# Attention and a state-space convolution on one core: transfers planned with their issue time, K's first weights moved, zero matmuls that fill every loop step

## The chip, the cores and the metric

The kernel runs on one core of a Trainium2 chip. The metric is the device time of one execution in microseconds (us), taken as the median of several runs. TensorE (PE) multiplies matrices, VectorE (DVE) and ScalarE (ACT) work on elements, GpSimd (POOL) sets a few buffers, and SyncE (SP) does nothing here but issue transfers. SP's own queue is shown as SPq.

## The reference

Two branches work on the same x (2048 positions, 512 channels) and are mixed by a gate:

```python
g = sigmoid((x * gate_w).sum(-1, keepdims=True))
# a: attention, 32 heads of 16 channels
q, k, v = split(x @ wqkv); p = softmax(q @ k.T * 16**-0.5); a = (p @ v) @ wo
# b: diagonal state-space convolution, 128 states per channel
dt = exp(log_dt); P = exp(dt * (A_re + 1j*A_im) * l)          # l = 0..2047
K = einsum("dn,dnl,dn->dl", C, P, dt * B).real
b = causal_convolution(x, K) + x * Dskip
return g * a + (1 - g) * b
```

## The kernel before

**The loop.** Attention is a loop of 683 steps over score tiles of 128 x 1536 (three of 128 x 512 each). Step t issues one exponential on ACT (`ex`, L679 to L682, the instruction at L681 that reads a score buffer SC and writes ET), and on TensorE the score matmuls for step t + 2 (`fill`, L661). SC has two buffers, so ACT has one tile in hand while TensorE fills the next. Value matmuls (`pv`, L684) accumulate into OA. One block of heads takes 16 key tiles, some 21 steps; then OA is moved out by VectorE (`norm`, L700) before the next block may open it. ET holds six tiles, so value matmuls can lag a little.

**The convolution** is done in chunks of 64 positions, as side work between the attention's instructions, by generators ("threads") with priorities: `params` and `bases` compute powers on VectorE; `table` writes tables PT and stores them to HBM; `qload` (L895, transfer at L899) reads them back transposed into Qt; `sstage` multiplies Qt with blocks of x into the PSUM bank MB, VectorE moves MB to Sst (L937), a transfer (L940) stores it, and `sload` (L960) reads it back transposed into SG; `scan` runs the recurrence on VectorE (L979 to L989); `kstage` makes the convolution kernels (Kst, stored at L917); `yload` (Py at L1004, four Tt loads at L1009) and `ystage` make the output from Tt, Py and SG in MB, stored at L1050 and read back transposed at L1065; `combine` and `outs` gate it and add the output projection. MB is one bank under a lock: a thread asks for it, works, and hands it back (`unlock`) as soon as the eviction to VectorE has been issued in the plan.

**The planner.** The order of all instructions is fixed when the program is built. `Prog.put` (L174) appends an operation to its engine's list and books its start and end on a model of the engines: `c` is its duration (for a transfer, time from issue to landing), `LAT` the delay of a semaphore. For a transfer the queue is booked like this (L194):

```python
if o.dma:
    self.free[eng] = t + .12
    e = t + o.c
```

`Sched.run` (L311) looks in each step for side operations whose operands are due in time by that model and appends them. TensorE, VectorE and the queues then run their lists in order on the chip: an operation that waits holds back all behind it on its engine.

**Zero matmuls.** `keep` (L696) multiplies zeros (the buffer wm) and adds them to OA, so that TensorE stays at work. At the end of each step they are appended until the step's TensorE work (`sch.units`) reaches 3.2 units of some 0.22 us, if a value accumulation is open (`opened`) and the model has room:

```python
while opened and sch.units < 3.2 and p.free["PE"] + .3 < lim:
    put(keep((pvn - 1) // 16))
    sch.units += 1
```

**Head.** Before the loop, ACT's queue issues x's first rows (x0n), log_dt (ldt), and the first columns of the weights Wk and Wq; SP's queue issues the transposed loads AreT and AimT, then Wv and the rest. TensorE runs nine zero matmuls, transposes x0n (L1181), ACT and VectorE copy the result to xT (L1192), then the first projections follow. ACT also computes dt, ea, e2 and a sine and cosine (L1193 to L1202) ahead of the loop.

**Placement.** `place` (L450) gives every buffer its bytes; buffers whose lifetimes in the plan don't meet may share bytes, and then the later one waits for the earlier one's last use.

Of the kernel before, what the change touches and what calls it, by code (L numbers as in the profile page):

```python
# [12 lines left out]
P = 128  # L13
# [54 lines left out]
class Prog:  # L68
# [179 lines left out]
class Sched:  # L248
# [62 lines left out]
    def run(self, now, pe_end, dve_end, margin=.02):  # L311
        p = self.p
        self.control()
        while True:
            best = None
            holder = [t for t in self.thr if t in self.lock.values()]
            for th in holder + [t for t in self.thr if t not in holder]:
                ops = th[3]
                if ops is None or isinstance(ops, tuple):
                    continue  # L320
                r = p.ready(ops)
                if r is None:
                    continue
                eng = ops[0].eng
                f = p.free[eng]
                if ops[0].dma:
                    if r > pe_end:
                        continue
                    k = 0
                elif eng == "PE":  # L330
                    c = sum(o.c for o in ops)
                    if max(f, r) + c > pe_end:
                        continue
                    k = 0 if r <= f + .03 else 2
                elif eng == "DVE":
                    if max(f, r) > dve_end:
                        continue
                    k = 0 if r <= f + .03 else 1 if r <= f + .16 else 2
                else:
                    if r > now:  # L340
                        continue
                    k = 0
                key = (k, r if k == 2 else 0)
                if best is None or key < best[0]:
                    best = (key, th)
                if k == 0:
                    break
# [102 lines left out]
def place(nc, bufs):  # L450
# [3 lines left out]

    def fit(order):
        done, top = [], base
        for b in order:
            n = (b.nbytes() + 31) // 32 * 32
            busy = sorted((o.lo, o.hi) for o in done if o.first <= b.last + 1 and b.first <= o.last + 1)
            at = base  # L460
            for lo, hi in busy:
                if at + n <= lo:
                    break
                at = max(at, hi)
            b.lo, b.hi = at, at + n
            top = max(top, b.hi)
            done.append(b)
        return top
# [3 lines left out]
    def rnd():  # L472
        nonlocal seed
        seed = (seed * 1103515245 + 12345) % 2 ** 31
        return seed / 2 ** 31

    best = None
    for k in range(200):
        def rank(b):
            w = rnd() * (0 if k < 2 else .8)  # L480
            return (-(b.last - b.first > 300) if k % 2 else 0, -b.nbytes() * (1 + w * 2) * (b.last - b.first + 20) ** (w if k >= 2 else 0))
        order = sorted(sbs, key=rank)
        top = fit(order)
        if best is None or top < best[0]:
            best = (top, order)
        if best[0] <= end:
            break
    for k in range(3000):
        if best[0] <= end:
            break  # L490
        order = list(best[1])
        order.insert(int(rnd() * len(order)), order.pop(int(rnd() * len(order))))
        top = fit(order)
        if top <= best[0]:
            best = (top, order)
    assert best[0] <= end, (best[0] - end, live(sbs))
    fit(best[1])
# [35 lines left out]
def record(p, B, ins):  # L533
# [21 lines left out]
    def dma(eng, fn, R, W, c):  # L555
        return O(eng, fn, R, W, c, dma=True)
# [10 lines left out]
    def load_xT(c):  # L567
        return dma("SP", lambda e: e.dma_start_transpose(xT(512 * c, [[S, 4], [1, 512]]),
                                                         dap(x_t, 512 * c * D, [[D, 512], [1, D]])), [], [(xT, c)], [0, 9, 15, 18][c])

    def load_par(n, src, c):
        return dma("SP", lambda e: e.dma_start_transpose(B[n](0, [[1, D]]), src), [], [(B[n], 0)], c)

    def load_w(n, c0, at, cols, sl, eng, c):
# [9 lines left out]
        load_w("Wv", 2 * D, 0, D, 0, "SP", 10),  # L584
        load_xT(1),
        load_w("Wk", D, P, D - P, 1, "SP", 15),
        load_w("Wq", 0, P, D - P, 1, "SP", 16),
        load_xT(2),
        load_xT(3))
    for n, s in (("BreT", "bre"), ("BimT", "bim"), ("CreT", "cre"), ("CimT", "cim")):  # L590
        put(load_par(n, ins[s], 24))
    put(dma("SP", lambda e: e.dma_start(B["gwT"](0, [[1, 4]]), dap(ins["gw"], 0, [[1, P], [P, 4]]), allow_slow_non_contiguous=True),
            [], [(B["gwT"], 0)], 27))
    for a in range(4):
        put(dma("SP", lambda e, a=a: e.dma_start(B["Dpb"](0, [[1, 16]], 32 * a, 32), dap(ins["dsk"], 0, [[1, 16], [256, 2], [16, 16]]),
                                                 allow_slow_non_contiguous=True), [], [(B["Dpb"], a)], 28))
# [156 lines left out]
    def params():  # L753
# [49 lines left out]

        yield [tt(full("u1"), half(L1, 0), full("e2"), ALU.mult, key("L1", "e2"), key("u1"))]
# [51 lines left out]
    def table():  # L856
# [5 lines left out]
        for pb in range(NBLK // 2):  # L862
# [21 lines left out]
            for i, blk in enumerate(blks):  # L884
                yield [dma("SP", lambda e, i=i, blk=blk: e.dma_start(ptd.dram(blk * P * PTN, [[PTN, P], [1, PTN]]), PT(i * PTN, [[1, PTN]])),
                           [W[i]], [(ptd, blk)], 6.0)]
# [8 lines left out]
    def qload(blk):  # L895
        if blk >= 2:
# [3 lines left out]
                                                         ptd.dram(blk * P * PTN, [[PTN, P], [1, PTN]])), [(ptd, blk)], [(Qt, blk % 2, blk)], 9.0)]  # L900
        sch.add(sstage(blk), 7)

    def kstage(blk):
# [4 lines left out]
        for part, wn in ((0, "wrb"), (1, "nwi")):  # L908
# [9 lines left out]
                   [(Kst, blk % 2, blk), (Kst, "z")], [(kpd, blk)], 4.5)]  # L918
# [4 lines left out]
    def sstage(blk):  # L923
        q0, qr, bl = (blk % 2) * PTN, blk // 4, blk % 4
        for bank in range(4):
            yield ("LOCK", "MB")
            os = []
            for pp in range(2):
                for j in range(4):
# [12 lines left out]
                       [(sd, (blk, bank))], 3.0)]  # L942
# [5 lines left out]
    def sload(blk):  # L948
# [7 lines left out]
        if bl == 0:  # L956
            yield [pool(lambda g: g.memset(sg(0, [[1, 2 * RS]]), 0.0), [], [(sg, "z")], 256)]
            if qr < 2:
# [3 lines left out]
                   [(sd, (blk, i)) for i in range(4)], [(sg, bl, (qr, 'S'))], 7.0)]  # L962
# [38 lines left out]
    def yload(u):  # L1001
# [4 lines left out]
                   [(ptd, blk)], [(Py, r, u)], 6.0)]  # L1006
        for par in range(2):
            for a in range(2):
# [3 lines left out]
                           [(kpd, blk)], [(Tt, (r, par, a), u)], 5.0)]  # L1012
        sch.mark(f"yl{u}")

    def ystage():
        def unit(u):
# [11 lines left out]
            for qq in range(2):  # L1028
# [9 lines left out]
                for q in (2 * qq, 2 * qq + 1):  # L1038
                    for ri in range(2):
# [11 lines left out]
                       [(Yst, r2, u)], [(ytd, u)], 2.6)]  # L1051
# [12 lines left out]
    def yread(blk):  # L1064
        yield [dma("SP", lambda e: e.dma_start_transpose(Yl(CB * blk, [[D, 16], [1, CB]]), ytd.dram(CB * blk * S, [[S, CB], [1, S]])),  # L1065
                   [(ytd, 2 * blk), (ytd, 2 * blk + 1)], [(Yl, blk)], 3.6)]
# [3 lines left out]
    def ublocks():  # L1070
# [3 lines left out]
        for qr in range(4):  # L1074
            yield ("Q", 30 + 10 * qr)
            for par in range(2):
                yield [dma("SP", lambda e, qr=qr, par=par: e.dma_start(X2(2048 * qr, [[64, 32], [1, 64]], 64 * par, 64),
                                                                       B["xrd"].dram(64 * qr + 256 * par, [[32 * D, 64], [D, 32], [1, 64]])),
                           [(B["xrd"], 0)], [(X2, (qr, par))], 7)]
# [45 lines left out]
    def out_st(lt):  # L1125
        return dma("SP", lambda e: e.dma_start(dap(ins["out"], 128 * lt * D, [[D, P], [1, D]]), fo((lt % 4) * D, [[1, D]])),
                   [(fo, lt % 4)], [(B["d_out"], lt)], 2.5)
# [65 lines left out]
    put(O("ACT", lambda a: a.activation(B["dt"](0, [[1, D]]), B["ldt"](0, [[1, D]]), AF.Exp), key("ldt"), key("dt"), .55))  # L1193
    put(tt(full("an"), full("AreT"), full("dt"), ALU.mult, key("AreT", "dt"), key("an")),
# [4 lines left out]
        O("ACT", lambda a: a.activation(B["e2"](0, PERM), B["an"](0, NAT), AF.Exp, scale=-2.0), key("an"), key("e2"), .55),  # L1199
# [37 lines left out]
    def pvs(t, limit):  # L1237
        nonlocal pvn, opened
        done = 0
        while pvn < NQ and (4 * pvn + 3) // W3 <= t and done < 2:  # L1240
# [19 lines left out]
            if not must and (r is None or r > p.free["PE"] + .03 or p.free["PE"] + .33 > limit):  # L1260
# [13 lines left out]
    for t in range(NT):  # L1274
# [27 lines left out]
        while opened and sch.units < 3.2 and p.free["PE"] + .3 < lim:  # L1302
            put(keep((pvn - 1) // 16))
# [5 lines left out]
    while True:  # L1309
        pvs(NT, 1e9)  # L1310
        if pvn >= NQ - 1:
            break
    sch.run(1e9, 1e9, 1e9)
# [47 lines left out]
```

## Time and profile before

| what | us |
|---|---|
| median of 3 runs (lowest, highest) | 1022.89 (1021.15, 1026.08) |
| the profiled execution | 1019.5 |
| its span, first to last instruction | 1017.4 |
| TensorE busy | 890.5 |
| ScalarE busy | 934.6 |
| VectorE busy | 605.8 |
| mean granted TensorE clock | 0.906 of full |

The busy times are unions over the whole span; they don't say which engine ended the waits in which stage. In views by stage each row has the stretch, its length, the busy time of each engine with its number of instructions, the granted clock, the share of the DMA engines and the rate. In the list of waits a row reads: who waited, for whom, total, times, longest. In rows in order of time: start, duration, engine, line, operation, tiles, count, and in brackets the idle time ahead and what ended it.

### The profile page before, as it was taken

To read this page: it belongs to the slowest core of one execution; us is meant where nothing else is said; L and a number is where in the kernel's file an instruction comes from. 1 tells how busy PE (TensorE), PEld (TensorE's weight loads), DVE (VectorE), ACT (ScalarE), POOL (GpSimd) and SP (SyncE) were. 2 spreads that over 40 slices of the span, in tenths; PEclk is the share of its full clock that TensorE was granted. 3 is DMA by queue.
4 is the path that set the end of the run, shared out by engine and by line. 5 is a ranking of instruction groups with operands and counts; after the bars stand their busy time and mean duration, and the time that the engine had idled before them with its cause. 6 is when DMAs were issued, how large, how long until landed. Compare 5 with 4: busy or idle time off the path is not lost.

```text
span 1017.4 us, 17925 instructions
## 1 busy us (share of the span) xinstructions
PE 890.5 (88%) x7623; PEld 261.4 (26%) x7623; DVE 605.8 (60%) x1315; ACT 934.6 (92%) x694; POOL 8.4 (1%) x17
## 2 busy tenths in 40 slices
PE   7999998889888888698899885988998999888887
PEld 2222222222222222122122332324233222222222
DVE  6999899972289998399972214799861420000001
ACT  6999999999799999699999964899897999999996
POOL 2000000000000000000000000000000000000000
PEclk9999989989799999889788965699795999999999
DMA  8710000076448417761653689835516100000000
GB/s 180 142 25 1 1 1 1 1 207 181 84 139 223 115 48 181 200 117 42 191 154 91 175 182 186 170 73 120 131 34 135 42 27 1 1 1 1 1 1 21
DMA packets 227406, 92.25 MB, mean 91 GB/s; under 512 B 191872, under 2 KB 215040, under 8 KB 225280
## 3 DMA queue, kind: packets, MB, share of 16 engines
q1 hardware_dynamic: 225600, 90.21, 37.0%
q10 hardware_dynamic: 1728, 0.92, 0.4%
q8 instruction: 59, 0.97, 0.4%
q14 instruction: 19, 0.16, 0.1%
HBM read 27.92 MB, written 35.65 MB: 62 GB/s over the span
## 4 chain that ended last, share of the span: by engine, by line
ACT 50%; PE 17%; DVE 15%; SPq 10%; DMA 5%; issue 1%; ACTq 0%; DVEq 0%
ACT ET L681 48%; PE OA L547 8%; PE SC L547 5%; PE MB L547 4%; SPq L1009 3%; DVE tt L712 3%; ACT EX L681 2%; DMA Qt<-gm_ptd 2%; SPq L960 2%; SPq L899 2%; DMA Tt<-gm_kpd 2%; DVE G L987 2%; DVE Sst L937 1%; DVE s L981 1%; DVE s L985 1%; DVE PT L712 1%
## 5 line engine op out<-in xcount | busy, mean ns | idle before, releaser
L681 ACT ACTIVATE ET<-SC 128x1536 bf16<-128x1536 f32 x665 | 902.8, 1598 | 68.1 <-PE SC L547 67.4
L547 PE MATMUL SC<-Qm,KT 32*128 32x512 bf16 x2048 | 285.3, 412 | 68.5 <-ACT ET L681 49.6
L547 PE MATMUL OA<-wm 128*128 128x512 bf16 x1015 | 324.6, 409 | 1.2 <-DVE wm L606 1.2
L547 PE MATMUL OA<-ET,VE 128*32 128x512 bf16 x1994 | 212.1, 420 | 0.0
L547 PEld LDWEIGHTS SC<-Qm,KT 32*128 32x128 bf16 x2048 | 67.0, 92 | 357.1 <-ACT ET L681 281.2
L702 DVE STREAM_TRANSPOSE OT<-OA 128x512 f32<-128x512 f32 x32 | 22.8, 713 | 193.6 <-PE OA L547 193.5
L547 PEld LDWEIGHTS OA<-wm 128*128 128x128 bf16 x1015 | 65.7, 99 | 132.6 <-issue 118.6
L937 DVE TENSOR_TENSOR Sst<-MB,sgn 128x512 bf16<-128x512 f32 x64 | 43.9, 686 | 65.9 <-PE MB L547 39.1
L547 PEld LDWEIGHTS OA<-ET,VE 128*32 128x32 bf16 x1994 | 51.1, 94 | 124.4 <-issue 120.8
L712 DVE TENSOR_TENSOR tt<-B,D 128x1024 bf16<-128x1024 bf16 x96 | 62.0, 680 | 0.5
L987 DVE TENSOR_TENSOR G<-s,s 128x256 f32<-128x256 f32 x120 | 50.5, 421 | 3.0
L1048 DVE CAST Yst<-MB 128x256 bf16<-128x256 f32 x32 | 13.5, 423 | 64.6 <-PE MB L547 59.5
L981 DVE TENSOR_TENSOR s<-G,MU 128x256 f32<-128x256 f32 x120 | 49.9, 416 | 0.1
L983 DVE TENSOR_TENSOR s<-G,MU 128x256 f32<-128x256 f32 x120 | 49.9, 416 | 0.0
L985 DVE TENSOR_TENSOR s<-s,SG 128x256 f32<-128x256 f32 x120 | 49.8, 415 | 0.0
L547 PE MATMUL MB<-Qt,X 64*32 64x256 bf16 x512 | 31.5, 326 | 18.7 <-DVE Sst L937 12.3
L547 PE MATMUL MB<-Tt,X 64*32 64x64 bf16 x512 | 25.1, 246 | 25.4 <-DMA Tt<-gm_kpd 24.5
L989 DVE CAST SG<-G 128x256 bf16<-128x256 f32 x120 | 34.7, 289 | 3.2
L712 DVE TENSOR_TENSOR ft<-FP,L 128x1024 f32<-128x1024 f32 (+1 forms) x32 | 33.7, 1082 | 0.4
L712 DVE TENSOR_TENSOR PT<-tt,tt 128x1024 bf16<-128x1024 bf16 x48 | 32.7, 682 | 0.6
L547 PE MATMUL MB<-Py,SG 128*32 128x64 bf16 x1024 | 29.6, 244 | 0.0
L547 PEld LDWEIGHTS MB<-Tt,X 64*32 64x32 bf16 x512 | 15.7, 145 | 48.5 <-DMA Tt<-gm_kpd 32.7
(131 smaller groups left out, 423.0 us busy)
## 6 DMA issues: line engine op xcount, KB each, us to landing
gm_ptd<-PT SPq DMA_DIRECT2D x16, 1024.0 KB, 5.7
Py<-gm_ptd SPq DMA_DIRECT2D x32, 512.0 KB, 4.5
gm_sd<-Sst SPq DMA_DIRECT2D x64, 128.0 KB, 1.8
gm_kpd<-Kst SPq DMA_DIRECT2D x16, 256.0 KB, 3.5
Tt<-gm_kpd SPq DMA_DIRECT2D x128, 32.0 KB, 3.6
gm_xrd<-in_A_x_dram SPq DMA_DIRECT2D x1, 2048.0 KB, 11.8
X<-gm_xrd SPq DMA_DIRECT2D x8, 256.0 KB, 6.1
gm_ytd<-Yst SPq DMA_DIRECT2D x32, 64.0 KB, 2.5
```

The source lines that it names most:

```text
L547: return O("PE", lambda t: t.matmul(out(), lhsT(), rhs(), start=start, stop=stop, skip_group_check=True, **kw), R, W, c, l, u)
L681: return ac(lambda a: a.activation(b(1536 * e, [[1, 512 * n]]), sc(0, [[1, 512 * n]]), AF.Exp, scale=DH ** -0.5), [(sc, k, (t, k)) for k i ...
L702: yield [dv(lambda v: v.transpose(OT(0, [[1, 512]]), OA(0, [[1, 512]])), [(OA, 0, b)], [(OT, 0, b)], 560)]
L712: return dv(lambda v: v.tensor_tensor(o(), a(), b_(), f), R, W, n, k)
L899: yield [dma("SP", lambda e: e.dma_start_transpose(Qt((blk % 2) * PTN, [[128, 32], [1, 128]]), ptd.dram(blk * P * PTN, [[PTN, P], [1, PTN] ...
L937: yield [dv(lambda v, bank=bank: v.tensor_tensor(Sst(512 * bank, [[1, 512]]), MB(0, [[1, 512]]), sgn(0, [[1, 512]]), ALU.mult), [(MB, 0, ( ...
L981: yield [dv(lambda v: v.tensor_tensor(s2(0, V2), G(0, V2), MU(d0, [[0, 2], [1, 128]]), ALU.mult), key("G", "MU"), [(s2, 0)], 256)]
L983: yield [dv(lambda v: v.tensor_tensor(s3(0, V2), G(128, [[-128, 2], [1, 128]]), MU(D + d0, [[D, 2], [1, 128]]), ALU.mult), key("G", "MU") ...
L985: yield [dv(lambda v, so=so: v.tensor_tensor(s2(0, V2), s2(0, V2), sg(so, [[RS, 2], [1, 128]]), ALU.add), [(s2, 0)] + ks, [(s2, 0)], 256)]
L987: yield [dv(lambda v: v.tensor_tensor(G(0, F), s2(0, F), s3(0, F), ALU.add), [(s2, 0), (s3, 0)], [(G, 0)], 256)]
L989: yield [dv(lambda v, so=so: v.tensor_copy(sg(so, [[RS, 2], [1, 128]]), G(0, V2)), key("G"), last, 256, 2)]
L1009: yield [dma("SP", lambda e, par=par, a=a: e.dma_start(Tt(r * 512 + 256 * a, [[64, 4], [1, 64]], 64 * par, 64), kpd.dram(blk * P * 8 * P + ...
```

## The change

- The model of a queue: every transfer books its queue for a time `u` of its own kind (0.6 us by default) in place of 0.12 us for all, and most landing times `c` are set anew. A transfer is only appended when the modelled queue is free by the end of the step. `emit` counts `u` as TensorE work for TensorE's operations alone.
- `ready` refuses a write into a place that holds something not yet read.
- Head: Wk's first columns go to SP's queue, ahead of AreT and AimT; Wq's move up to third on ACT's. Five zero matmuls are put behind the transposes of x0n. On ACT, dt's exponential goes ahead of the two copies; e2 is no longer an exponential of ACT, but a product and a reciprocal on VectorE, in `params` after the mark "D48".
- `keep` can also write into MB, as a matmul of its own. A step is topped up to 3.2 units when an accumulation is open, as before, and now also when none is open and nobody holds MB.
- At the end, value matmuls are appended without regard to the model's time, and side work is run between them.
- `place` searches for a placement in another way.

```diff
-                for b, sl, *_ in acc:
+                for b, sl, *tag in acc:
...
+                    if wr and tag and not st[1] and b.tags.get(sl, "warm") not in ("warm", tag[0]):
+                        return None
...
-            self.free[eng] = t + .12
+            self.free[eng] = t + o.u
...
-            self.units += o.u
+            if o.eng == "PE":
+                self.units += o.u
...
-                    if r > pe_end:
+                    if max(r, f) > pe_end:
...
-    def dma(eng, fn, R, W, c):
-        return O(eng, fn, R, W, c, dma=True)
+    def dma(eng, fn, R, W, c, u=.6):
+        return O(eng, fn, R, W, c, u=u, dma=True)
...
-        load_w("Wk", D, 0, P, 0, "ACT", 6.8),
-        load_w("Wq", 0, 0, P, 0, "ACT", 8.0),
+        load_w("Wq", 0, 0, P, 0, "ACT", 6.5),
+        load_w("Wk", D, 0, P, 0, "SP", 7.0),
...
     def keep(b):
-        return mm(lambda: OA(0, [[1, 512]]), lambda: wm(0, [[1, P]]), lambda: wm(0, [[1, 512]]), [(wm, 0)], [(OA, 0, b)],
-                  False, False, c=.24)
+        o = MB if b is None else OA
+        return mm(lambda: o(0, [[1, 512]]), lambda: wm(0, [[1, P]]), lambda: wm(0, [[1, 512]]), [(wm, 0)],
+                  [(o, 0, "warm" if b is None else b)], b is None, b is None, c=.24)
...
+        yield [tt(perm("u1"), nat("ea"), nat("ea"), ALU.mult, key("ea"), key("u1"))]
+        yield [dv(lambda v: v.reciprocal(B["e2"](0, [[1, D]]), B["u1"](0, [[1, D]])), key("u1"), key("e2"), 3050)]
...
-    put(copy_dve(*cp[0]), copy_act(*cp[1]), copy_dve(*cp[2]), copy_act(*cp[3]))
+    put(*[mm(lambda: OA(0, [[1, 512]]), lambda: wm(0, [[1, 128]]), lambda: wm(0, [[1, 512]]), [(wm, 0)], [(OA, 0, "warm")], c=.22)
+          for k in range(5)])
+    put(copy_dve(*cp[0]), copy_dve(*cp[2]))
     put(O("ACT", lambda a: a.activation(B["dt"](0, [[1, D]]), B["ldt"](0, [[1, D]]), AF.Exp), key("ldt"), key("dt"), .55))
+    put(copy_act(*cp[1]), copy_act(*cp[3]))
...
-        O("ACT", lambda a: a.activation(B["e2"](0, PERM), B["an"](0, NAT), AF.Exp, scale=-2.0), key("an"), key("e2"), .55),
...
-            if not must and (r is None or r > p.free["PE"] + .03 or p.free["PE"] + .33 > limit):
+            if not must and limit < 1e8 and (r is None or r > p.free["PE"] + .03 or p.free["PE"] + .33 > limit):
...
-        while opened and sch.units < 3.2 and p.free["PE"] + .3 < lim:
-            put(keep((pvn - 1) // 16))
+        while sch.units < 3.2 and p.free["PE"] + .3 < lim and (opened or sch.lock.get("MB") is None):
+            put(keep((pvn - 1) // 16 if opened else None))
```

Charges of the main transfers, issue to landing `c` and queue time `u`, in us (before, every `u` was 0.12):

| transfer | c before | c after | u after |
|---|---|---|---|
| PT to HBM | 6.0 | 6.5 | 0.5 |
| Qt, transposed (L899) | 9.0 | 10.5 | 5.6 |
| Kst to HBM | 4.5 | 4.5 | 0.4 |
| Sst to HBM (L940) | 3.0 | 2.7 | 0.45 |
| SG, transposed (L960) | 7.0 | 6.3 | 2.6 |
| Py (L1004) | 6.0 | 5.5 | 0.65 |
| Tt, four a unit (L1009) | 5.0 | 4.6 | 0.68 |
| Yst to HBM (L1050) | 2.6 | 3.3 | 0.65 |
| Yl, transposed (L1065) | 3.6 | 3.8 | 1.35 |

More of the change, by code (lines that the diff above doesn't have):

```diff
@@ L453, in place @@
     sbs = [b for b in bufs.values() if b.kind == "sb" and b.first is not None]
+    size = {b: (b.nbytes() + 31) // 32 * 32 for b in sbs}
+    conf = {b: [o for o in sbs if o is not b and o.first <= b.last + 1 and b.first <= o.last + 1] for b in sbs}
     def fit(order):
-        done, top = [], base
+        over = 0
+        for b in sbs:
+            b.lo = None
         for b in order:
-            n = (b.nbytes() + 31) // 32 * 32
-            busy = sorted((o.lo, o.hi) for o in done if o.first <= b.last + 1 and b.first <= o.last + 1)
@@ L460, in fit @@
             at = base
-            for lo, hi in busy:
-                if at + n <= lo:
+            for lo, hi in sorted((o.lo, o.lo + size[o]) for o in conf[b] if o.lo is not None):
+                if at + size[b] <= lo:
                     break
                 at = max(at, hi)
[L465 to L468, printed above, removed]
+            b.lo, b.hi = at, at + size[b]
+            over += max(0, b.hi - end)
+        return over
@@ L470, in place, with rnd @@
     seed = 1
-    def rnd():
+    def rnd(n):
         nonlocal seed
         seed = (seed * 1103515245 + 12345) % 2 ** 31
[L475 to L486, printed above, removed]
-            break
@@ L488, in place @@
[L488 to L497, printed above, removed]
+        return (seed >> 8) % n
+    first = sorted(sbs, key=lambda b: -(b.last - b.first + 30) * size[b])
+    for k in range(24000):
+        if k % 4000 == 0:
+            order, best = first, None
+        o = list(order)
+        if best is not None:
+            x = out[rnd(len(out))] if rnd(10) < 6 else o[rnd(len(o))]
+            o.remove(x)
+            o.insert(rnd(len(o)), x)
+        over = fit(o)
+        if best is None or over <= best:
+            order, best, out = o, over, [b for b in sbs if b.hi > end]
+        if best == 0:
+            break
@@ L498, in place @@
+    assert best == 0, (best, live(sbs))
+    fit(order)
     for b in sbs:
@@ L579, in record @@
         load("ACT", B["ldt"], lambda: dap(ins["ldt"], 0, [[0, P], [1, D]]), [(B["ldt"], 0)], [[1, D]], 0, 6.2),
-        load_w("Wk", D, 0, P, 0, "ACT", 6.8),
-        load_w("Wq", 0, 0, P, 0, "ACT", 8.0),
+        load_w("Wq", 0, 0, P, 0, "ACT", 6.5),
+        load_w("Wk", D, 0, P, 0, "SP", 7.0),
         load_par("AreT", ins["are"], 6.6),
         load_par("AimT", ins["aim"], 7.5),
-        load_w("Wv", 2 * D, 0, D, 0, "SP", 10),
+        load_w("Wv", 2 * D, 0, D, 0, "SP", 6.5),
         load_xT(1),
-        load_w("Wk", D, P, D - P, 1, "SP", 15),
-        load_w("Wq", 0, P, D - P, 1, "SP", 16),
+        load_w("Wk", D, P, D - P, 1, "SP", 4.5),
+        load_w("Wq", 0, P, D - P, 1, "SP", 5),
         load_xT(2),
@@ L961, in sload @@
                                                          sd.dram(CB * blk * 8192, [[8192, CB], [1, 8192]])),
-                   [(sd, (blk, i)) for i in range(4)], [(sg, bl, (qr, 'S'))], 7.0)]
+                   [(sd, (blk, i)) for i in range(4)], [(sg, bl, (qr, 'S'))], 6.3, 2.6)]
         sch.mark(f"sg{blk}")
@@ L1312, in record @@
             break
+        sch.run(1e9, 1e9, 1e9)
     sch.run(1e9, 1e9, 1e9)
```

30 lines of the change are left out of this document (15 added, 15 removed).

## The prediction

> **What bounds the kernel now.** I read the page first, then the list of waits, then the busy time by stages, then single stalls in order of time.
>
> The page: span, granted TensorE clock in 40 slices, and ScalarE's exponentials, which with 902.8 us of busy time are the longest job.
>
> ```profile
> span 1017.4 us, 17925 instructions
> PEclk9999989989799999889788965699795999999999
> L681 ACT ACTIVATE ET<-SC 128x1536 bf16<-128x1536 f32 x665 | 902.8, 1598 | 68.1 <-PE SC L547 67.4
> ```
>
> ScalarE (ACT) sets the pace: 902.8 / 665 = 1.358 us a tile, and 68.1 us of idle time ahead of them, nearly all ended by score matmuls (SC). So the most that better feeding can bring is near 68 us. The clock row falls to 0.5 to 0.7 in some slices. The list of waits says who makes the score matmuls late (total us, times, longest):
>
> ```profile
> ACT ET L681 <- PE SC L547: 67.4, 74, 9.9
> DVE Sst L937 <- DMA gm_sd<-Sst: 26.4, 8, 8.6
> PE MB L547 <- DMA Tt<-gm_kpd: 24.5, 20, 9.4
> DVE G L979 <- DMA SG<-gm_sd: 20.4, 2, 12.5
> PE MB L547 <- DVE Sst L937: 13.8, 12, 5.9
> PE MB L547 <- DMA Qt<-gm_ptd: 5.9, 4, 2.3
> ```
>
> TensorE takes its matmuls in program order, so one matmul of the convolution (into MB) that waits for a transfer holds back the score matmuls behind it. Transfers hold TensorE directly for 24.5 + 5.9 us, and another 13.8 us by way of VectorE, which itself waits for transfers (Sst, G). The stages show where (length, busy time of PE, PEld, DVE, ACT, POOL, clock, DMA share, GB/s):
>
> ```profile
> 0.00:25.40 25.40, 19.33 (x89) 7.34 (x89) 16.18 (x34) 17.51 (x18) 5.29 (x11) 0.93 0.85 181
> 25.40:203.50 178.10, 166.79 (x1190) 46.55 (x1190) 171.74 (x258) 177.47 (x134) 0.00 (x0) 0.97 0.14 25
> 203.50:254.30 50.80, 45.59 (x361) 12.07 (x361) 26.43 (x46) 49.43 (x38) 1.23 (x2) 0.91 0.71 194
> 254.30:280.00 25.70, 21.77 (x166) 5.43 (x162) 5.10 (x8) 19.23 (x15) 0.00 (x0) 0.71 0.43 84
> 280.00:405.00 125.00, 108.31 (x901) 29.85 (x901) 116.92 (x279) 124.43 (x94) 0.00 (x0) 0.99 0.52 140
> 405.00:437.00 32.00, 22.08 (x175) 5.84 (x173) 14.43 (x32) 21.64 (x16) 1.23 (x2) 0.84 0.78 190
> 437.00:550.00 113.00, 100.52 (x796) 26.85 (x792) 91.02 (x222) 107.17 (x79) 0.00 (x0) 0.88 0.48 125
> ...
> 583.00:656.00 73.00, 54.94 (x742) 20.43 (x739) 29.29 (x83) 45.80 (x33) 0.68 (x2) 0.58 0.85 177
> ...
> 703.00:790.00 87.00, 77.49 (x965) 27.73 (x962) 49.77 (x140) 74.37 (x55) 0.00 (x0) 0.76 0.48 106
> 790.00:1000.00 210.00, 189.76 (x1280) 49.22 (x1279) 26.76 (x59) 209.08 (x156) 0.00 (x0) 0.98 0.03 8
> 1000.00:1017.40 17.40, 11.98 (x72) 3.75 (x68) 4.83 (x8) 8.50 (x7) 0.00 (x0) 0.98 0.09 30
> ```
>
> Length less ACT's busy time is ACT's idle time. Head 7.89, tail 8.90. The stages from 254.3 to 790 that use the DMA engines: 6.47 + 0.57 + 10.36 + 5.83 + 27.20 + 12.63 = 63.06 us. The attention stretches beside them (25.4 to 254.3 and 790 to 1000): 0.63 + 1.37 + 0.92 = 2.92. Low clock and ACT's idle time stand in the same stages. The worst stall, with SyncE's queue (SPq) ahead of it and the stretch behind it:
>
> ```profile
> 606.77 7.34 SPq L960 DMA_TRANSPOSE SG<-gm_sd  x3
> 614.80 2.69 SPq L1009 DMA_DIRECT2D Tt<-gm_kpd  x4
> 619.39 0.26 PE L547 MATMUL MB<-Tt,X 64*32 64x64 bf16 x1 [9.42 <-DMA Tt<-gm_kpd]
> 621.80:655.00 33.20, 29.42 (x378) 10.31 (x374) 24.48 (x71) 24.10 (x17) 0.34 (x1) 0.50 0.78 166
> ```
>
> Three transposes occupied the queue for 7.34 us, the four Tt loads were issued behind them, and TensorE stood for 9.42 us. Then the clock was granted at 0.50 for 33.2 us, in which ACT lost another 33.20 - 24.10 = 9.1 us. A late transfer is paid twice.
>
> **The change part by part.** (1) Issue times. The planner charged the issuing queue 0.12 us a transfer; now it charges by kind, and holds a transfer back while its model of the queue is full. What the chip took (issue ns min/median/max), and the median from issue to landing, last figure of the lower rows:
>
> ```profile
> L899 SPq DMA_TRANSPOSE Qt<-gm_ptd x16: 4642/5005/7073, 211.8 to 533.6; - x16
> L960 SPq DMA_TRANSPOSE SG<-gm_sd x16: 1427/2421/4359, 247.4 to 664.9; - x16
> L1009 SPq DMA_DIRECT2D Tt<-gm_kpd x128: 603/617/1674, 558.7 to 780.1; - x128
> Tt<-gm_kpd SPq DMA_DIRECT2D x128, 32.0 KB, 3.6
> Qt<-gm_ptd SPq DMA_TRANSPOSE x16, 8.2
> SG<-gm_sd SPq DMA_TRANSPOSE x16, 5.0
> ```
>
> Old against new charge: Qt 0.12 to 5.6 (measured 5.0), SG 0.12 to 2.6 (2.4), Tt 0.12 to 0.68 (0.62); landing Qt 9.0 to 10.5 (8.2), SG 7.0 to 6.3 (5.0), Tt 5.0 to 4.6 (3.6). Each new figure lies a little above the median. In the stall above the old model counted 3 x 0.12 us for the transposes and 4 x 0.12 for Tt, 0.84 us against 7.34 + 2.69 = 10.03; the 9.19 us it left out is the 9.42 us that TensorE stood. The new one counts 3 x 2.6 + 4 x 0.68 = 10.5. The matmuls on Tt, Qt and SG should therefore be placed behind score and value matmuls, not ahead of them. The chip's transfers get no quicker; the wait moves from TensorE into the convolution's own chain. Worth: between 63.1 us (all idle time of these stages) and 31.5 us (half, if the maxima such as 7.07 and 4.36 us still surprise the plan). I take 54, residue 9: the new figures cover the median of every kind, and only the tail of the distribution and VectorE's lateness are left. Nearer to the upper end since the deficit of the worst stall is met almost to the digit.
>
> What is late next: the convolution. It ended here:
>
> ```profile
> 822.29 0.97 PE MB L547 x4
> ```
>
> ACT has 8.50 us of work after 1000 in the last stage, so the exponentials end near 1008.5; with 57 us gone they would end near 951, and the convolution (823.3) has some 128 us of cover.
>
> (2) Filling. Before, zero matmuls topped a step up to 3.2 only while a value accumulation was open; now also between two blocks of heads, into MB when nobody holds it. The border at 837 us:
>
> ```profile
> 835.90:839.30 3.40, 1.83 (x18) 0.56 (x19) 2.34 (x5) 3.40 (x3) 0.00 (x0) 1.00 0.00 0
> 839.30:842.70 3.40, 3.40 (x14) 0.49 (x14) 0.00 (x0) 3.25 (x3) 0.00 (x0) 0.50 0.02 5
> ```
>
> TensorE was busy for 1.83 of 3.40 us, and in the next 3.40 the clock was 0.50. Filling that removes such drops can bring at most the 2.92 us of the attention stretches. It can also cost: the first filler after an eviction of MB waits for VectorE, in order, ahead of the next scores; ACT has a tile in hand (1.358 us), so I bound this at -2 us. I take a gain of 1.5. By the Trainium skill (TensorE: Matmul & The Clock Gate, Part 1) the clock halves after a window of about 3.4 us in which TensorE was idle; the two rows disagree in part, since 1.83 us of work lay in the window ahead of the drop. By that rule the fillers at a border would bring nothing, and the sum would be 1.5 us longer.
>
> (3) Head. K's first weights go to SyncE's queue, Q's move up in ACT's; five zero matmuls keep TensorE busy; dt's exponential goes ahead of ACT's two copies; ACT's e2 becomes a VectorE product and a reciprocal.
>
> ```profile
> 1.73 0.46 ACTq L563 DMA_DIRECT2D Wk<-in_A_wqkv_dram  x1
> Wk<-in_A_wqkv_dram ACTq DMA_DIRECT2D x1, 128.0 KB, 6.1
> 6.10 1.26 ACT L1187 CAST xT<-SC 128x512 bf16<-128x512 f32 x2 [1.99 <-PE SC L547]
> 7.26 0.63 ACT L1193 ACTIVATE dt<-ldt 128x512 bf16<-128x512 bf16 x1
> 9.49 1.60 PE L547 MATMUL OA<-xT,Wq 128*128 128x512 bf16 x4 [2.76 <-DMA Wq<-in_A_wqkv_dram]
> 15.18 1.45 ACT L681 ACTIVATE ET<-SC 128x1536 bf16<-128x1536 f32 x1 [1.43 <-PE SC L547]
> ```
>
> Q's weights ended a 2.76 us wait of TensorE at 9.49. In K's old place they would be issued at 1.73 and land at 1.73 + 6.1 = 7.83, 1.7 us sooner. The copies, behind dt, end some 0.63 us or more later than their 7.36, so the projection can't finish before about 8.5. The fillers start at the end of the transposes (9.49 - 2.76 = 6.73) and end by then. SyncE's AreT, AimT and Wv each start one short issue (about 0.5 us) later. I take a gain of 1.8 at the first exponential; ends 2.8 (the whole wait) and a loss of 1.0 (ACT's copies late). By the Trainium skill (Trainium Kernel Development and Optimization, Key Constraints) queues of several engines share the 16 DMA engines, and issuing from more of them saves only issue time; no row here separates the two, and by that rule the gain would be 0.46 us, the sum 1.3 us longer.
>
> (4) The reciprocal. The only row is small:
>
> ```profile
> L703 DVE RECIPROCAL Rz<-OT 128x16 f32<-128x16 f32 x32 | 7.8, 245 | 0.3
> ```
>
> 512 columns cost between 0.25 us and 32 x 0.245 = 7.8 us; I take 3.3, between, near what the code books. With the product some 4 us of VectorE, which is full in 25.4 to 203.5 (171.74 of 178.10): the convolution starts 4 us later, hidden by its cover of 128 us. Without that cover it would cost its 4 us. (5) Placement of buffers, the guard in ready() and the last value matmuls: none issues anything new on ACT's path; 0, with +-1 for the tail's 8.90 us. The plain `emit` change only keeps queue time out of TensorE's units: 0.
>
> Sum: 1017.4 - 54 - 1.5 - 1.8 = 960.1 us of span. The profiled execution took 1019.5, 2.1 more than its span: 962.2. The median of the runs (1022.89) lies 3.4 above that execution; I add half, since part of that scatter is in stalls that go: 964.
>
> **The rivals.** *Half the stalls stay (about 988).* The plan is open-loop: a Qt issue of 7.07 us against 5.6 planned, or VectorE late behind one landing, halts TensorE as before and the clock falls. For: longest against median in the issue rows. Against: they are few. 1017.4 - 31.5 - 1 + 2.1 = 987, with the runs' scatter 988.
>
> *Slower: the convolution outlasts attention.* Transfers are now placed later, each landing planned above its median: Qt by 2.3 us in 16 blocks, a Tt group by some 1.25 us (3 x 0.06 in issue, 1.0 in landing) in 32 units: 37 + 40 = 77 us if all of it fell on one chain. 823 + 77 = 900 is still ahead of 951, and the output products behind it fit. It decides from 128 us on; twice that slip, 154 us, gives 1017.4 - 57 + 26 + 8 of a longer tail = 994, and only a slip of over 190 us, from transfers held back while the lock on MB blocks all others, passes 1023: say 1050.
>
> *The order hardly changes (about 1016).* If most waits came from VectorE and not from queue time, only head and borders are gained and given back. Against: 9.19 us left out against 9.42 waited.
>
> *The two rules of the Trainium skill hold.* Both small gains shrink, by 1.5 and 1.3: 967. The drop after 1.83 us of work speaks against the one.
>
> **How the numbers follow.** The forecast (964) 0.68; the Trainium skill's rules 0.09 (967); half 0.15 (988); hardly changed 0.04; slower 0.04. The range: best end 1017.4 - 63.1 - 2.9 - 2.8 + 2.1 = 950.7, rounded to 949; upper end 989, the half case. About 0.15 lies outside. Five us (0.5%) is what a measurement of this kernel can tell from no change. Faster 0.93, same 0.03, slower 0.04.
>
> **What would show it.** Right: waits of MB's matmuls for Tt and Qt fall from 30 us to under 6; ACT's idle time ahead of the exponentials from 68 to 10 or 15; the clock from 0.906 to 0.97 or more; the first exponential near 13.4 us; no 0.50 row at a border in the stretch without DMA. Wrong: MB waits of several us in the same stages, a clock under 0.95, convolution matmuls within 20 us of the end, or a filler that waits for VectorE ahead of scores.

## The result and the profile after

The changed kernel takes 957.05 us (median of four runs, 954.06 to 959.24) against 1022.96 for the kernel before in the same runs: a ratio of 0.9351, 95% interval 0.9313 to 0.9388. In a later series the same pair gave 955.87 and 1022.43, ratio 0.9351 (0.9316 to 0.9386). The forecast was 964, range 949 to 989.

The page of the changed kernel (span, clock in 40 slices, the exponentials) and then its list of waits (who, for whom, total, times, longest):

```profile
span 952.3 us, 17960 instructions
PEclk9999989999999999999899999999999999999999
L681 ACT ACTIVATE ET<-SC 128x1536 bf16<-128x1536 f32 x665 | 896.5, 1724 | 10.0 <-PE SC L547 9.4
```

```profile
PE MB L547 <- DVE Sst L940: 11.2, 16, 3.0
ACT ET L681 <- PE SC L547: 9.4, 18, 2.4
DVE G L982 <- DMA SG<-gm_sd: 3.0, 1, 3.0
PE MB L547 <- DMA Tt<-gm_kpd: 2.3, 5, 0.9
```

ScalarE's idle time ahead of the exponentials went from 68.1 to 10.0 us. TensorE's direct waits on Tt went from 24.5 to 2.3 us, and no wait on Qt is left in the list (5.9 before). What remains is mostly VectorE moving MB to Sst (11.2 against 13.8). The stages, in the same columns and nearly the same stretches as before:

```profile
254.30:280.00 25.70, 21.56 (x202) 6.59 (x203) 7.10 (x12) 25.70 (x20) 0.00 (x0) 0.95 0.40 91
405.00:437.00 32.00, 25.39 (x221) 7.41 (x224) 21.63 (x39) 29.11 (x23) 1.23 (x2) 0.96 0.92 221
437.00:550.00 113.00, 99.01 (x811) 28.19 (x821) 91.68 (x226) 111.27 (x83) 0.00 (x0) 0.95 0.48 126
583.00:656.00 73.00, 66.42 (x994) 28.25 (x1007) 32.05 (x91) 70.95 (x54) 0.34 (x1) 0.98 0.79 165
703.00:790.00 87.00, 78.94 (x1072) 31.11 (x1083) 52.86 (x152) 86.73 (x66) 0.00 (x0) 1.00 0.48 107
```

In 583 to 656 ScalarE now works for 70.95 of 73.00 us (45.80 before), with the DMA engines nearly as busy (0.79 against 0.85). The transfers themselves did not get quicker. This is SyncE's queue of the changed kernel in that stage, in order of time:

```profile
616.97 10.33 SPq L963 DMA_TRANSPOSE SG<-gm_sd  x4
627.40 1.22 SPq L1068 DMA_TRANSPOSE Yl<-gm_ytd  x1
628.67 0.59 SPq L1007 DMA_DIRECT2D Py<-gm_ptd  x1
629.30 2.59 SPq L1012 DMA_DIRECT2D Tt<-gm_kpd  x4
```

Four SG transposes hold the queue for 10.33 us, longer than the three before (7.34 us), and the Tt loads are issued behind them as before. But TensorE has other matmuls in its list meanwhile: the first matmul that waits for a Tt behind these transposes stands at 633.99 and waits 0.32 us, where 9.42 us were lost before.

Where the 65.1 us of span went: ScalarE's idle time after its first exponential fell from 66.7 (68.1 less 1.43 ahead of the first) to 10.0, so 56.7; the first exponential starts at 12.34 instead of 15.18, 2.8; the 665 exponentials of the large group took 896.5 instead of 902.8 us, 6.3; together 65.8, and the tail is some 0.5 longer. Most of the 6.3 us is a price of the waits themselves. Two rows of the kernel before show it, a run of ten exponentials and one that came after a wait:

```profile
828.97 13.57 ACT L681 ACTIVATE ET<-SC 128x1536 bf16<-128x1536 f32 x10
842.88 1.45 ACT L681 ACTIVATE ET<-SC 128x1536 bf16<-128x1536 f32 x1 [0.33 <-PE SC L547]
```

One alone takes 1.45 us; ten take 13.57, which is 1.45 + 9 x 1.347. So every wait costs some 0.10 us on top of its idle time. The list of waits has 74 before and 18 after: 56 x 0.10 = 5.8 us. The Trainium skill (ScalarE: Activation LUTs, What ACT_TABLE_LOAD costs) says that back-to-back ACTIVATEs overlap by about 93 ns; the rows agree.

### The profile page after: what moved, and what is told of

Read it like the earlier page. It is cut to its first block, busy times and chain, and to the rows that moved or that the text cites. A ratio compares the mean times of both kernels' runs of the same rounds, so it can differ in the third digit from the quotient of the medians.

```text
span 952.3 us, 17960 instructions
## 1 busy us (share of the span) xinstructions
PE 845.2 (89%) x7580; PEld 263.1 (28%) x7706; DVE 611.8 (64%) x1317; ACT 927.7 (97%) x693; POOL 8.4 (1%) x17
## 4 chain that ended last, share of the span: by engine, by line
ACT 56%; DVE 20%; PE 12%; SPq 6%; DMA 4%; issue 2%; DVEq 0%; ACTq 0%
ACT ET L681 53%; PE OA L547 5%; PE SC L547 4%; PE MB L547 3%; DVE tt L713 3%; ACT EX L681 3%; SPq L963 2%; DVE G L990 2%; DVE s L988 2%; DVE s L984 2%; SPq L1012 2%; DVE s L986 2%; DVE PT L713 1%; DVE SG L992 1%; DVE Sst L940 1%
## 5 line engine op out<-in xcount | busy, mean ns | idle before, releaser
L681 ACT ACTIVATE ET<-SC 128x1536 bf16<-128x1536 f32 x665 | 896.5, 1724 | 10.0 <-PE SC L547 9.4
L547 PE MATMUL SC<-Qm,KT 32*128 32x512 bf16 x2048 | 271.5, 391 | 63.6 <-ACT ET L681 39.7
L547 PE MATMUL OA<-wm 128*128 128x512 bf16 x921 | 285.7, 392 | 16.1 <-issue 14.9
L547 PE MATMUL OA<-ET,VE 128*32 128x512 bf16 x1994 | 201.3, 398 | 0.1
L940 DVE TENSOR_TENSOR Sst<-MB,sgn 128x512 bf16<-128x512 f32 x64 | 43.8, 685 | 65.5 <-PE MB L547 46.2
L547 PE MATMUL MB<-Qt,X 64*32 64x256 bf16 x512 | 29.4, 306 | 9.4 <-DVE Sst L940 9.2
L681 ACT ACTIVATE EX<-SC 128x1536 bf16<-128x1536 f32 x18 | 24.3, 1546 | 0.1
L547 PE MATMUL MB<-Tt,X 64*32 64x64 bf16 x512 | 21.5, 235 | 3.1 <-DMA Tt<-gm_kpd 2.3
```

Source lines behind the costliest of these rows:

```text
L547: return O("PE", lambda t: t.matmul(out(), lhsT(), rhs(), start=start, stop=stop, skip_group_check=True, **kw), R, W, c, l, u)
L681: return ac(lambda a: a.activation(b(1536 * e, [[1, 512 * n]]), sc(0, [[1, 512 * n]]), AF.Exp, scale=DH ** -0.5), [(sc, k, (t, k)) for k i ...
L940: yield [dv(lambda v, bank=bank: v.tensor_tensor(Sst(512 * bank, [[1, 512]]), MB(0, [[1, 512]]), sgn(0, [[1, 512]]), ALU.mult), [(MB, 0, ( ...
```

## The experiments

Three theories were set against each other: Q, that the time came from transfers planned with their queue time; F, that it came from the zero matmuls and the clock; H, that it came from the head. Line numbers of variants are their own. All edits are to the changed kernel.

**The queue model alone** (old head, no zero matmuls into MB):

```diff
-        while sch.units < 3.2 and p.free["PE"] + .3 < lim and (opened or sch.lock.get("MB") is None):
+        while sch.units < 3.2 and p.free["PE"] + .3 < lim and opened:
...
-        load_w("Wq", 0, 0, P, 0, "ACT", 6.5),
-        load_w("Wk", D, 0, P, 0, "SP", 7.0),
+        load_w("Wk", D, 0, P, 0, "ACT", 6.8),
+        load_w("Wq", 0, 0, P, 0, "ACT", 8.0),
```

(and ACT's order, e2 and the five zero matmuls left out, as before.) Expected:

> The changed kernel with the old head (K's first weights on ACT's queue, dt behind the copies, no five zero matmuls, e2 on ACT) and without zero matmuls into MB: of the change, the queue times, the landing times and the hold of a full queue are left (and the new placement and the guard). Theory Q (the time came from transfers planned with their queue time): 959 to 964 us, waits of MB's matmuls for Tt and Qt of a few us. Rival F (the time came from the zero matmuls, which keep the clock up): 1000 us or more, the clock near 0.91. Rival H (the head sets off a better order): 990 or more.

Measured: 965.47 us (961.98 to 967.27), ratio 0.946 (0.9435 to 0.9485). The queue model alone, with the placement and the guard that stayed in, brings 55 to 56 of the 66 us: Q. F and H fall.

**Everything but the queue model:**

```diff
-            self.free[eng] = t + o.u
+            self.free[eng] = t + .12
...
-                    if max(r, f) > pe_end:
+                    if r > pe_end:
...
-                                                         ptd.dram(blk * P * PTN, [[PTN, P], [1, PTN]])), [(ptd, blk)], [(Qt, blk % 2, blk)], 10.5, 5.6)]
+                                                         ptd.dram(blk * P * PTN, [[PTN, P], [1, PTN]])), [(ptd, blk)], [(Qt, blk % 2, blk)], 9.0)]
```

(and so on for every transfer.)

> The changed kernel with the old model of the queue: 0.12 us for every transfer, the old landing times, no hold. Head, zero matmuls into MB, placement and guard stay as changed. Theory Q: most of the gain is gone, 1005 to 1020 us, TensorE waits 25 us or more for Tt and Qt and the clock is near 0.91. Rival F: 960 to 970 us, the clock 0.96 or more.

Measured: 1024.78 us, ratio 1.0028 (1.0006 to 1.005), a little above the range of Q. Without the queue model the rest of the change, placement and guard included, brings nothing. Its list of waits:

```profile
ACT ET L681 <- PE SC L547: 74.5, 72, 12.9
PE MB L547 <- DVE Sst L940: 26.8, 18, 13.0
PE MB L547 <- DMA Tt<-gm_kpd: 22.5, 19, 6.5
```

The waits of the kernel before are back, the longest now 13.0 us.

**Which half of the model?** First the new landing times with the old queue time and no hold, then the new queue times and the hold with the old landing times of the convolution's transfers:

```diff
-            self.free[eng] = t + o.u
+            self.free[eng] = t + .12
...
-                    if max(r, f) > pe_end:
+                    if r > pe_end:
```

> The changed kernel with 0.12 us of queue time for every transfer and no hold of a full queue; the new landing times stay. Theory U: 1005 to 1030 us, TensorE waiting 40 us or more on MB's matmuls, as with the whole old model (59 us there). Rival L: 955 to 970.

```diff
-                                                         ptd.dram(blk * P * PTN, [[PTN, P], [1, PTN]])), [(ptd, blk)], [(Qt, blk % 2, blk)], 10.5, 5.6)]
+                                                         ptd.dram(blk * P * PTN, [[PTN, P], [1, PTN]])), [(ptd, blk)], [(Qt, blk % 2, blk)], 9.0, 5.6)]
...
-                           [(kpd, blk)], [(Tt, (r, par, a), u)], 4.6, .68)]
+                           [(kpd, blk)], [(Tt, (r, par, a), u)], 5.0, .68)]
```

(and the other six transfers likewise.)

> The changed kernel with the old landing times for the convolution's transfers (PT 6.0, Qt 9.0, Sst 3.0, SG 7.0, Py 6.0, Tt 5.0, Yst 2.6, Yl 3.6); new queue times and the hold stay. Theory U (the queue time is what the old model lacked): 955 to 964 us. Rival L (the new landing times do it): 990 or more.

Measured: landing times only, 1033.21 us, ratio 1.0099 (1.0065 to 1.0132), slower than the kernel before; queue times only, 964.61 us, ratio 0.9433 (0.9403 to 0.9463). The queue time and the hold together are what the old model lacked; which of the two does it was not tried. The 8.7 us that queue times alone stay behind the changed kernel (955.87 in the same series) are not all the landing times': the first exponential came 2.2 us later there (14.60 against 12.40, see the last section). Several new landing times are shorter than the old (SG 6.3 for 7.0, Tt 4.6 for 5.0), and alone they make the plan worse; a possible reason is that the old ones held part of the queue's delay, which was not tried.

**The dose: a few transfers planned too early.** Two runs; in the first Qt of blocks 5, 9 and 13, in the second of 4, 8 and 12:

```diff
-                                                         ptd.dram(blk * P * PTN, [[PTN, P], [1, PTN]])), [(ptd, blk)], [(Qt, blk % 2, blk)], 10.5, 5.6)]
+                                                         ptd.dram(blk * P * PTN, [[PTN, P], [1, PTN]])), [(ptd, blk)], [(Qt, blk % 2, blk)], 3.5 if blk in (4, 8, 12) else 10.5, 5.6)]
```

> The changed kernel with Qt's landing planned at 3.5 instead of 10.5 us for blocks 5, 9 and 13 alone; the chip took 7.8, so each of the three reads is placed up to 4.3 us too early. Theory T (a late transfer is paid twice, once as TensorE's wait and again at the halved clock behind it): three waits of 2 to 5 us, each with a clock of 0.5 for 3.4 us or more behind it; 8 to 15 us more than the changed kernel. Rival O (paid once): the wait less the tile that ACT has in hand, 3 to 9 us more in all and no fall of the clock. Rival N (TensorE's other work ahead covers it): within 2 us.

> The changed kernel with Qt's landing planned at 3.5 instead of 10.5 us for blocks 4, 8 and 12, which are read 2 to 4 us after their landing in the changed kernel (blocks 5, 9 and 13, taken first, were read 12 us after theirs, so that their early plan had no effect). Theory T (paid twice): three waits of 1.5 to 5 us on Qt, each with the clock at 0.5 behind it for 3.4 us or more; 6 to 15 us more than the changed kernel. Rival O (paid once): ACT's idle time grows by less than the waits themselves, the clock does not fall; 2 to 6 us. Rival N: within 2 us, no waits on Qt.

Measured: 957.67 us (954.41 to 962.58) for the odd blocks: no effect (rival N). The odd block of a pair waits for MB behind the even one: at 334.07 its matmuls had stood 2.17 us for VectorE, not for Qt. For the even blocks 974.91 us (967.53 to 978.09), ratio 0.9502 (0.9462 to 0.9543), against 955.87 of the changed kernel on the chip of the odd blocks' run. The three waits and ScalarE's first exponential behind each, in the second run:

```profile
315.09 0.46 PE L547 MATMUL MB<-Qt,X 64*32 64x256 bf16 x8 [2.61 <-DMA Qt<-gm_ptd]
317.12 1.45 ACT L681 ACTIVATE ET<-SC 128x1536 bf16<-128x1536 f32 x1 [2.39 <-PE SC L547]
412.74 0.66 PE L547 MATMUL MB<-Qt,X 64*32 64x256 bf16 x8 [5.47 <-DMA Qt<-gm_ptd]
414.95 1.45 ACT L681 ACTIVATE ET<-SC 128x1536 bf16<-128x1536 f32 x1 [5.44 <-PE SC L547]
486.96 0.65 PE L547 MATMUL MB<-Qt,X 64*32 64x256 bf16 x8 [3.15 <-DMA Qt<-gm_ptd]
488.74 1.45 ACT L681 ACTIVATE ET<-SC 128x1536 bf16<-128x1536 f32 x1 [3.02 <-PE SC L547]
```

TensorE waited 11.2 us in all and ScalarE stood for 10.9 us behind it: a late transfer is paid almost in full, the tile that ScalarE has in hand covers hardly any of it. Behind the three waits the clock was granted at 0.51 to 0.54 for 3.4 to 6 us, and ScalarE stood another 0.51 us after the first, 0.61 after the second and 0.60 + 0.64 after the third, 2.4 us in all. So a second payment is there at these three places, but small. Of the rest of the 19 us, 4.7 fell in one later stretch at a clock of 0.50, shown below; the remainder lies in other stages of a plan that differs.

**The zero matmuls.** Without those into MB, without any in the loop, and filled to 3.6:

```diff
-        while sch.units < 3.2 and p.free["PE"] + .3 < lim and (opened or sch.lock.get("MB") is None):
+        while sch.units < 3.2 and p.free["PE"] + .3 < lim and opened:
```

> The changed kernel with zero matmuls only while a value accumulation is open, as before. Theory Q: 958 to 961 us (fillers worth 1 to 3 us), low clock again at borders of the stretch without transfers. By the Trainium skill (TensorE: Matmul & The Clock Gate, Part 1: a window of some 3.4 us without work halves the clock) no difference, 956 to 958. Rival F: over 975.

```diff
+        while False and (opened or sch.lock.get("MB") is None):
```

> The changed kernel without any zero matmul in the loop; the head's stay. Theory K (the loop's zero matmuls hold the clock): the clock at 0.5 for most of the loop; at half clock a step's score and value matmuls take 0.61 + 0.62 us of 1.35, and a convolution group 0.65 more, so only steps with side work are late: 1020 to 1120 us. Rival: the loop's own work holds the clock well enough and the planner, with TensorE freer, loses nothing: 950 to 970 us.

```diff
+        while sch.units < 3.6 and p.free["PE"] + .3 < lim and (opened or sch.lock.get("MB") is None):
```

> The changed kernel with steps filled to 3.6 units instead of 3.2. If more filling keeps the clock from falling: half the low-clock time (46 us) and 951 to 955. If the extra work makes TensorE itself late, most of all where the clock is already low: 960 to 985. Else 954 to 959.

Measured: 964.51 us without MB's (ratio 0.9439, 0.9403 to 0.9474); 964.16 with none in the loop (0.9418, 0.9391 to 0.9445); 956.25 filled to 3.6 (0.9339, 0.9313 to 0.9366), no difference. The stretch of attention without transfers, in the changed kernel and without MB's fillers:

```profile
790.00:930.00 140.00, 126.89 (x861) 34.01 (x875) 20.26 (x43) 139.98 (x105) 0.00 (x0) 1.00 0.04 12
```

```profile
790.00:930.00 140.00, 126.03 (x843) 32.55 (x842) 22.51 (x49) 138.75 (x104) 0.00 (x0) 0.96 0.04 12
893.70:900.60 6.90, 6.86 (x33) 1.20 (x31) 0.00 (x0) 5.83 (x5) 0.00 (x0) 0.51 0.00 0
```

The fillers do hold the clock at the borders (1.00 against 0.96), worth 1.2 us in this stretch. The second row is one such drop: at 0.51 ScalarE works for 5.83 of 6.90 us. The kernel with no zero matmul in the loop was the surprise; its clock, and the stage that was worst before:

```profile
core 0: 960.2 us, clock 0.598
583.00:656.00 73.00, 68.31 (x927) 24.13 (x924) 28.77 (x82) 71.58 (x54) 0.34 (x1) 0.50 0.77 166
```

At a clock of 0.50 ScalarE works for 71.58 of 73.00 us, as well as the changed kernel at 0.98 (70.95), and far better than the kernel before at 0.58 (45.80). The whole loop at little over half clock, without its zero matmuls, takes some 7 to 8 us of 957 more. So a low clock by itself costs little here. It is another matter when zero matmuls fill the steps. In the run with the even blocks planned early, a later stretch ran at 0.50 (first row: all work; second row: the zero matmuls alone, busy time of PE, PEld and DVE):

```profile
639.70:663.60 23.90, 23.90 (x262) 7.49 (x258) 19.47 (x58) 19.20 (x14) 0.00 (x0) 0.50 0.70 165
639.70:663.60 23.90, 7.48 (x15) 1.23 (x15) 0.00 (x0) 0.50 0.70 165
```

TensorE waited for no transfer there: it was busy for all of 23.90 us, 7.48 of them with fifteen zero matmuls, and ScalarE stood for 4.70. The plan counts 0.24 us for a zero matmul; at half clock two take 1.03, and a step of scores, values and two of them took 2.06 us (from the score matmuls at 646.37 to the next at 648.43) where ScalarE needs 1.35. One plan with and without zero matmuls at the same low clock was not tried, so how the price divides between clock and filling is argued from these rows.

**The head as before,** alone:

> The changed kernel with the old head and e2 on ACT. If the head's gain goes straight to the end: 959.5 to 961 us, the first exponential near 15.2 instead of 12.34 us. If it is hidden by the waits that are left: 957 to 958.

Measured: 963.95 us (960.8 to 965.77), ratio 0.9436 (0.9407 to 0.9465), the first exponential at 15.36. The first exponential is 3.0 us later than the changed kernel's 12.34; the other 4 to 5 us are idle time elsewhere, in a plan that came out another way. (The edit is the head's part of the first experiment's.) For the fillers it is the same: removed one at a time, head and fillers each cost 7 to 9 us, removed both 8 to 10. Without MB's fillers the first exponential stood at 13.88, 1.5 us later, though the head was not edited. Each edit gives a plan with its own leftover waits, and differences of under some 8 us between variants are not the edited part's alone. That may also be why several ranges given in advance for the favoured theory were missed by 1 to 5 us: the queue model alone, the old queue, the landing times alone, MB's fillers, the old head and the even blocks.

**The changed kernel once more,** for scale:

> The changed kernel itself once more, to have its time on the same chip as its variants. 955 to 962 us by every theory; how far its profile differs from the first one tells what a difference of a few us between variants is worth.

Measured: 955.87 us (954.43 to 957.28), span 952.7, 10.0 us of idle time ahead of the large group, as in the first profile (952.3 and 10.0). One kernel repeats well; it is the plans that differ.

**A more cautious plan:**

```diff
-            self.free[eng] = t + o.u
-            e = t + o.c
+            self.free[eng] = t + 1.25 * o.u
+            e = t + o.c + 1.0
```

> The changed kernel with every queue time raised by a quarter and every landing 1.0 us later in the plan. Theory M (the 10 us of ACT's idle time that are left are transfers later than planned): 948 to 953 us, waits of MB's matmuls under 8 us instead of 15 to 17. Rival V (they are VectorE's order, which a later landing does not mend): 954 to 960. Rival S (the convolution's chain gets too long): over 960.

Measured: 951.82 us (950.54 to 959.1), ratio 0.931 (0.928 to 0.9339). Its list of waits:

```profile
ACT ET L681 <- PE SC L547: 4.0, 11, 0.8
PE MB L547 <- DVE Sst L940: 2.1, 6, 0.8
```

The time is in the range of theory M, and of the waits for Sst, 11.2 us in the changed kernel, 2.1 are left. All waits of MB's matmuls in the list come to 10.7 us, though, not under 8; 4.5 of them are for fo, at the output projection. That the waits for Sst too came from transfers later than planned fits this, but isn't shown by itself: VectorE's own waits for the store of Sst hardly changed (17.3 us against 19.3), and TensorE's matmuls behind it now stand later. The interval overlaps that of the changed kernel (0.9313 to 0.9388), so the version is the lowest measured here but not shown to be faster.

## Why the prediction was right, point by point

- *Issue times.* Right, mechanism and place; the runs with half of the model show that the queue time and the hold carry it. Expected 54 us of the stages' 63 us. All idle time after the first exponential fell by 56.7 us, where the terms for stages and borders had 55.5. The first rival, that half of the stalls stay, did not come. That 9.19 us left out met 9.42 waited almost to the digit was partly luck: the load of Py between the two rows (0.60 us at 614.16, charged 0.12) was not counted, nor the 0.45 us that TensorE stood next for Tt. With both it is 9.67 against 9.87, at one stall alone.
- *A late transfer is paid twice.* Right only in part. I read the stretch from 621.8 to 655, with 9.1 us more idle time at a clock of 0.50, as the low clock's price. Two views of that stretch in the kernel before, TensorE's waits for Tt and the zero matmuls alone, divide it:

```profile
PE MB L547 <- DMA Tt<-gm_kpd: 3.2, 5, 2.0
621.80:655.00 33.20, 5.78 (x11) 0.75 (x11) 0.00 (x0) 0.50 0.78 166
```

Five further late Tt took 3.2 us of it. Almost all of the other 5.9 fell while TensorE was at work (29.42 of 33.20 us), 5.78 us of that on eleven zero matmuls at half clock. The kernel without zero matmuls does the stage at 0.50 and loses 1.4 us. A border drop shows the same price, 1.1 us in 6.9, where two zero matmuls at half clock (1.03 us) stand in a step beside scores and values (0.61 + 0.62): more than ScalarE's 1.35. So the second payment is real where the steps are filled, and the low clock alone does not make it. How much of it would be left with the old queue model and no zero matmuls was not tried.
- *Exponentials.* The term that the sum lacked: 6.3 us, since an exponential after a wait takes 1.45 instead of 1.35 us. Most of the gap between the 960.1 us of span in the sum and the 952.3 measured is this.
- *Filling.* Sized at 1.5 us; in 790 to 930 ScalarE stood 0.64 us in the kernel before, 0.02 in the changed one and 1.25 in the changed one without MB's fillers. By removal the whole kernel gained up to 8, part of which is the plan's. The clock drops came back without the fillers, at borders with no gap of 3.4 us: in the rows ahead of the drop at 893.7 the longest is 0.95. The Trainium skill (TensorE: Matmul & The Clock Gate, Part 1) names an idle window of about 3.4 us ahead of a drop; taken as a window without any work, as the prediction took it, these runs do not agree, and the rival built on that reading falls.
- *Head.* Sized at 1.8, measured 2.84, at the end I gave for it (2.8). Q's weights were issued at 1.88 instead of 2.22 and landed 5.5 us later instead of 7.2, at about 7.4 instead of 9.4. That is more than the 0.46 us of issue time, so the time forecast by the rival built on the Trainium skill (Trainium Kernel Development and Optimization, Key Constraints) did not come. The rule itself is not put to the test: the order of the loads changed too, and nothing here shows why they landed quicker.
- *Convolution's cover.* Right: its last matmuls of outputs in the loop end at 817.7, ScalarE's exponentials at 942.9.
- *The rival of the slower convolution.* It stayed away. Two slips in its working change nothing: 3 x 0.06 + 1.0 is 1.18, not 1.25, so 38 and not 40 us, and by its own sum a slip of some 180 us, not 190, passes 1023.
- *Scatter.* I added half of the 3.4 us between the profiled execution and the median; the profiled execution after (954.06) lies 3.0 below its median.

## What to carry to other kernels

When an order is planned against modelled times, the time that a queue needs to issue a transfer belongs in the model before anything else: one transposed load held the queue for 5 us where the plan had 0.12, and an in-order engine pays that lateness almost one to one. Look for the queue's rows directly ahead of the worst wait and add up what the plan left out; here 9.7 us against waits of 9.9. And when a low clock stands beside lost time, ask what fills the engine there: at 0.50 this program lost 1.4 of 73 us in a plan without zero matmuls, and 4.7 of 23.9 in a stretch filled with them for the full clock.

## What the runs showed of the hardware that was not expected

In the head, VectorE's small comparison of 128 x 128 elements took 2.55 us in the changed kernel and 4.82 in the cautious one. First the changed kernel, then the cautious one, each with the memset of GpSimd that ends just before it:

```profile
1.09 2.27 POOL L620 MEMSET VE<- 128x512 bf16 x1
1.10 2.55 DVE L607 TENSOR_SCALAR idb<-idf 128x128 bf16<-128x128 f32 x1
```

```profile
1.10 4.82 DVE L607 TENSOR_SCALAR idb<-idf 128x128 bf16<-128x128 f32 x1
4.03 1.80 POOL L624 MEMSET Kst<- 128x2048 bf16 x1
```

It ends 0.29 us after the first memset (3.36) in the one, and 0.09 us after the last of five (5.83) in the other. The Trainium skill (SBUF — State Buffer, Who interferes with whom) says that VectorE in a two-port mode and GpSimd hold a shared pair of ports for a whole instruction and block each other; the rows fit that, if this instruction ran in such a mode, which they don't show; it would then have been passed over several times in the second kernel. The first exponential came at 14.59 us in the cautious kernel, 2.2 us after the 12.34 of the changed one. In the profiled executions with the new head it took 4.82 us in four kernels (old queue, queue times alone, odd blocks, cautious), and their first exponential came at 14.59 or 14.60; in the others it took 2.55 or 2.56, and the first exponential came between 12.34 and 13.88. Why one execution waits for one memset and another for all is open, and so is what the cautious plan would take with the shorter wait.
